# Second attention and expert product of an inducing-point mixture-of-experts kernel: fp32 weights in 32-row tiles in place of a split into two block-diagonal halves

## The chip, the cores and the metric

The kernel runs on one core of a Trainium2 chip, in one launch. The metric is the device time in microseconds (us), as the median of several runs. One execution was taken by the hardware profiler; its durations are the ones used here. Engines are named as the profile names them: PE (TensorE, matrix products), PEld (its weight loads), DVE (VectorE), ACT (ScalarE), POOL (GpSimd), SP (SyncE, which issues the loads and stores).

## The reference, cut to what matters

```python
B, N, m, C = (4, 11456, 32, 128)          # x: B x N x C, inducing: m x C
def mab(q, kv):
    s = scale * (q @ kv.transpose(0, 2, 1))
    s = s - s.max(-1, keepdims=True)
    a = np.exp(s)
    a /= a.sum(-1, keepdims=True) + 1e-09
    return a @ kv
h = mab(I, x)                             # first attention: 32 inducing points over all tokens
out = mab(x, h)                           # second attention: every token over the 32 rows of h
...
logits = out @ w_gate                     # E = 8 experts, D = 128, F = 1024
expert_idx = np.argmax(logits, axis=1)
gate_w = softmax(logits)[arange, expert_idx]
y = gate_w * (np.maximum(out @ w1[e], 0.0) @ w2[e])    # e = the token's expert
```

All tensors are fp32. The output has 45824 rows of 128. Where all tokens of a batch choose one expert and no hidden unit changes its sign over them, the expert is a fixed matrix: y = gate * (a @ L). The kernel computes in this form, proves both conditions on the chip, and has a general path behind them.

## The kernel before, in words

Each of the four batches is cut into G = 6 groups: five of 16 tiles (a tile is 128 tokens, one per partition) and a last one of 10 (8 and a tail of 2). `p1(i)` (from L389) does the first attention of group i, `chain(b)` (from L480) joins a batch's groups into h and prepares its expert, and `p2(i)` (from L603) does the second attention and the expert for group i.

`p1`: each x tile is transposed on PE (L400) and copied to `xT` (L403, through the helper at L313). Scores come from four fp32 products side by side, each into 32 of the 128 output partitions (L416), then the maximum (L423, L427, L430), the exponential (L434), a 32 x 32 block transpose on DVE (L438) and the sum over tokens, again four products side by side (L445).

`chain`: h is normalised and transposed to `hT` (L511 to L515), the expert is chosen, its weights are fetched by an indirect DMA (L531), and out of them comes L, the 32 x 128 matrix with y = gate * (a @ L). Nine router columns join it, so that one product gives 128 columns of y, 8 logits and the sum of the weights: `WY` = 137. L590 spreads L over the partitions with `selq` into two block-diagonal halves `[128, 2, 137]`, and L593 and L594 split that into `Lh` (fp32r, the rounded part) and `Ll` (the rest). In the last batch the nine router columns stand apart, in `rr` (L556), since gates are wanted there before the expert is known.

`p2`: scores (L612), a block transpose (L615), maximum (L617), difference (L619) and exponential (L623) leave the unnormalised weights `sd`: per partition 16 tokens by 32. These are split into `eh[..., 0]`, rounded to fp32r (the copy of L627), and `eh[..., 1]`, the rest (the subtraction of L629, POOL or DVE). A pair of tiles, rounded and rest, fills 128 columns, so a group has 8 transposes (L642), whose results go to SBUF as `eT` in two copies of 512 columns (L644). For each pair `my` (L652) runs two products of 274 columns, with `Lh` (L653) and with `Ll` (L654): the rounded and the rest are summed over the 128 rows, and the block diagonal keeps the two tiles of the pair apart. In the first three batches each pair goes to `ys` (L695), `gates` (from L720) makes 1 / (sum * sum of exponentials), and L708 or L706 scales four tiles at a time into `yo`, which SP stores (L716). In the last batch a product with `rr` (L648) gives logits first (`sp_`, then `st` by an addition, L665), the products of 256 columns leave PSUM scaled (L686, L688), or through `ya` and POOL (L677, L679) for the first `XQ[g]` quads, and stores go out per four tiles. In the last batch the products of the later quads wait for the gates (L673).

The order of work is not written out by hand. Every operation is recorded in a `Plan` (L137) with the engines that could run it, a rough cost on each, the tiles it reads and writes, and a key. `emit` (L166) takes the operation that can start first, adding a bias per kind of operation (`BIAS`, L59); within `WINDOW` ns the smaller key wins (L249). PSUM is 8 banks handed out as they come free (`pick`, L230); SBUF tiles have as many slots as `BUFS` (L60) says. The result is a fixed order of instructions on each engine.

Of the kernel before, what the change touches and what calls it, by code (L numbers as in the profile page):

```python
# [59 lines left out]
BUFS = {"w1e": 1, "w2e": 1, "x": 6, "xT": 7, "eT": 1, "eh": 3, "sd": 6, "a": 1, "aT": 1, "ys": 2, "yo": 2}  # L60
# [3 lines left out]
def inducing_moe_kernel(ctx: ExitStack, tc: tile.TileContext, x, inducing, w_gate, w1, w2, out):  # L64
    nc = tc.nc
# [17 lines left out]
    ident_r = consts.tile([128, 128], F32R, name="ident_r")  # L83
    dve.tensor_copy(ident_r, ident)
# [14 lines left out]
    # selq[:, q]: the columns of sel4 whose r has r % 2 == q  # L99
    selq = consts.tile([128, 2, 128], F32, name="selq")  # L100
    dve.memset(selq, 0.0)
    for r in range(4):
        dve.tensor_copy(selq[:, r % 2, 32 * r:32 * r + 32], sel4[:, 32 * r:32 * r + 32])
    # mq[:, q]: the rows whose block r has r % 2 == q
    mq = consts.tile([128, 2], F32, name="mq")
    dve.memset(mq, 0.0)
    for r in range(4):
        dve.memset(mq[32 * r:32 * r + 32, r % 2:r % 2 + 1], 1.0)
    # far: 0 where sel4 is 1, else far below everything
# [10 lines left out]
    # per batch state that outlives the pipeline  # L120
# [3 lines left out]
    far_ = consts.tile([128, B * G], F32, name="far_")     # the largest logit_j - logit_e of a group, per partition  # L124
# [12 lines left out]
class Plan:  # L137
    """Orders the recorded operations over the engines: a list schedule with rough costs.

    An operation is given with the engines that could run it and its cost in ns on each.  It waits  # L140
    for the earlier writers of what it reads and for the earlier readers of what it writes.  A tile
    is allocated by its first writer: the slot of its tag (SBUF) or the bank (PSUM) that has been free for longest.
    """

    @staticmethod
    def edge(a, b):
        """ns from the end of an operation on engine a to the start of one on b that waits for it"""
        if a == "sp" or b == "sp":
            return 1200
        return 197 if a == "pe" else 185 if b == "pe" else 142  # L150

    WINDOW = 20

    def __init__(self):
        self.ops, self.tiles, self.pull = [], {}, []
# [4 lines left out]
    def op(self, engs, fn, r=(), w=(), key=0.0, hold=(), pull=0.0):  # L160
# [3 lines left out]
        self.pull.append(pull)  # L164

    def emit(self, bufs, banks, run):  # L166
# [39 lines left out]
        def slots(i):  # L206
            """the last users of the slots that operation i opens; None if not yet known"""
            t = []
            for x in self.ops[i][3] + self.ops[i][5]:
# [3 lines left out]
                if tag == "bank":  # L213
                    k = pick()
                    if k is None:
                        return None
# [694 lines left out]
```

## Time and profile before

| what | value |
|---|---|
| median of 3 runs | 239.0 us |
| lowest and highest run | 238.43 and 242.09 us |
| span of the profiled execution, first to last instruction | 239.8 us |
| PE, DVE, ACT, POOL busy, of the span | 88%, 81%, 70%, 44% |
| granted TensorE clock, mean | 0.970 |
| moved by DMA | 51.62 MB, 215 GB/s on the mean |

No other time is given for the profiled execution, so its span stands for its own time; it lies 0.8 us above the median and between the lowest and the highest run. Busy times of PE include the modelled tail of each burst, so the step from one start to the next on the timeline says more of what PE can do. The granted clock is the mean of a stretch between its two levels, 1.2 and 2.4 GHz, as a share of the higher.

### The profile page before, as it was taken

To read this page: it belongs to the slowest core of one execution; us is meant where nothing else is said; L and a number is where in the kernel's file an instruction comes from. 1 tells how busy PE (TensorE), PEld (TensorE's weight loads), DVE (VectorE), ACT (ScalarE), POOL (GpSimd) and SP (SyncE) were. 2 spreads that over 40 slices of the span, in tenths; PEclk is the share of its full clock that TensorE was granted. 3 is DMA by queue.
4 is the path that set the end of the run, shared out by engine and by line. 5 is a ranking of instruction groups with operands and counts; after the bars stand their busy time and mean duration, and the time that the engine had idled before them with its cause. 6 is when DMAs were issued, how large, how long until landed. Compare 5 with 4: busy or idle time off the path is not lost.

```text
span 239.8 us, 6157 instructions
## 1 busy us (share of the span) xinstructions
PE 211.9 (88%) x2245; PEld 154.7 (65%) x2245; DVE 194.9 (81%) x608; ACT 168.9 (70%) x444; POOL 105.3 (44%) x115
## 2 busy tenths in 40 slices
PE   8599999989988999898998999999999988598460
PEld 5366765567946756666777656668676555598460
DVE  5124477998799799899897989999999999979950
ACT  3278754879946899798866897688986868577310
POOL 2000002242364446193582558295556868645400
PEclk9999999999999999999999999999999999889766
DMA  6995795941549574857569671425404724475872
GB/s 197 352 406 205 269 361 185 306 168 53 175 174 342 213 284 150 305 189 316 178 230 403 210 251 68 179 87 195 175 3 175 242 111 178 176 257 212 316 259 59
DMA packets 12310, 51.62 MB, mean 215 GB/s; under 512 B 1616, under 2 KB 2672, under 8 KB 7920
## 3 DMA queue, kind: packets, MB, share of 16 engines
q1 hardware_dynamic: 11120, 46.95, 53.1%
q0 software_dynamic: 1152, 4.19, 5.5%
q8 instruction: 20, 0.33, 0.6%
q14 instruction: 18, 0.15, 0.2%
HBM read 27.68 MB, written 23.46 MB: 213 GB/s over the span
## 4 chain that ended last, share of the span: by engine, by line
PE 43%; DVE 39%; ACT 6%; DMA 4%; issue 4%; SPq 1%; POOL 0%; ACTq 0%; DVEq 0%
PE b L400 8%; PE b L653 8%; PE b L654 6%; PE b L445 5%; DVE sd L619 4%; PE b L416 4%; DMA x<-in_x_dram 4%; DVE yo L708 4%; PE b L612 4%; DVE sd L615 3%; PE b L642 3%; DVE mx L423 3%; DVE mx L617 3%; DVE aT L438 2%; ACT xT L313 2%
## 5 line engine op out<-in xcount | busy, mean ns | idle before, releaser
L708 POOL TENSOR_TENSOR yo<-ys,gs 128x512 f32<-128x512 f32 (+1 forms) x48 | 53.4, 1131 | 17.7 <-DVE gs L739 7.6
L313 ACT COPY xT<-b 128x512 f32<-128x512 f32 (+1 forms) x92 | 48.4, 588 | 16.8 <-PE b L400 15.6
L400 PE MATMUL b<-ident,x 128*128 128x128 f32 x352 | 48.3, 281 | 2.9 <-DMA x<-in_x_dram 2.9
L400 PEld LDWEIGHTS b<-ident,x 128*128 128x128 f32 x352 | 40.2, 145 | 13.1 <-issue 5.4
L629 POOL TENSOR_TENSOR eh<-sd,eh 128x512 fp32r<-128x512 f32 (+1 forms) x24 | 30.1, 1257 | 33.6 <-ACT eh L313 15.7
L313 ACT COPY ys<-b 128x274 f32<-128x274 f32 x111 | 36.4, 403 | 8.1 <-PE b L654 6.3
L653 PE MATMUL b<-Lh,eT 128*128 128x274 f32 x135 | 39.9, 319 | 2.0 <-DVE eT L313 1.4
L654 PE MATMUL b<-Ll,eT 128*128 128x274 f32 x135 | 36.0, 291 | 0.0
L653 PEld LDWEIGHTS b<-Lh,eT 128*128 128x128 f32 x135 | 25.8, 191 | 12.8 <-issue 5.1
L654 PEld LDWEIGHTS b<-Ll,eT 128*128 128x128 f32 x135 | 25.7, 191 | 0.0
L416 PE MATMUL b<-xT,IT 128*32 128x512 f32 (+2 forms) x192 | 24.1, 571 | 0.7 <-ACT xT L313 0.6
L445 PE MATMUL b<-x,aT 128*32 128x128 f32 x704 | 24.1, 275 | 0.2 <-DVE nb L430 0.2
L612 PE MATMUL b<-xT,hT 128*32 128x512 f32 (+1 forms) x192 | 23.7, 576 | 0.0
L531 POOL DMA_INDIRECT w1e<-in_moe_w_dram,idx x4 | 4.3, 1075 | 42.1 <-DVE idx L525 40.4
L619 DVE CUSTOM_DVE_ANT_0 sd<-mx,sd 128x512 f32<-128x512 f32 (+1 forms) x24 | 21.9, 913 | 0.1
L445 PEld LDWEIGHTS b<-x,aT 128*32 128x32 f32 x704 | 18.2, 109 | 5.1 <-issue 2.9
L642 PE MATMUL b<-ident_r,eh 128*128 128x128 f32 x180 | 19.7, 250 | 1.1 <-POOL eh L629 0.7
L642 PEld LDWEIGHTS b<-ident_r,eh 128*128 128x128 f32 x180 | 17.2, 140 | 4.6 <-issue 1.8
L423 DVE TENSOR_REDUCE mx<-b 128x1 f32<-128x512 f32 (+1 forms) x24 | 15.3, 639 | 5.7 <-PE b L416 5.5
L438 DVE STREAM_TRANSPOSE aT<-a 128x512 f32<-128x512 f32 (+1 forms) x24 | 16.1, 669 | 4.1 <-ACT a L434 3.7
L434 ACT ACTIVATE a<-b,nb 128x512 f32<-128x512 f32 (+1 forms) x24 | 16.2, 674 | 3.1 <-DVE nb L430 3.0
L653 PE MATMUL b<-Lh,x 128*128 128x256 f32 x45 | 15.2, 356 | 2.0 <-ACT x L313 2.0
(208 smaller groups left out, 391.6 us busy)
## 6 DMA issues: line engine op xcount, KB each, us to landing
x<-in_x_dram SPq DMA_DIRECT2D x19, 1024.0 KB, 6.4
out_dram<-yo SPq DMA_DIRECT2D x15, 1024.0 KB, 4.3
out_dram<-ys SPq DMA_DIRECT2D x12, 256.0 KB, 2.8
out_dram<-yo SPq DMA_DIRECT2D x10, 256.0 KB, 2.2
x<-in_x_dram SPq DMA_DIRECT2D x4, 512.0 KB, 6.2
out_dram<-yo SPq DMA_DIRECT2D x3, 512.0 KB, 3.1
x<-in_x_dram SPq DMA_DIRECT2D x4, 256.0 KB, 3.2
xtail<-in_x_dram SPq DMA_DIRECT2D x4, 64.0 KB, 6.4
```

The lines of the kernel that those rows point to most:

```text
L313: (eng.copy if eng is nc.scalar else eng.tensor_copy)(out, in_)
L400: e.transpose(T[t][:, k, :], xtile(i, t0 + k), ident) for k in range(n)],
L416: e.matmul(T[t][32 * k:32 * k + 32, :ends[k]], IT, T[xT][:, k, :ends[k]], start=True, stop=True) for k in range(4)],
L423: e.tensor_reduce(T[mx], T[t][:, :nt], axis=AX.XY, op=OP.max)
L445: e.matmul(T[th][32 * k:32 * k + 32, :], T[aT][:n, q + k], xtile(i, q + k)[:n], start=q == 0, stop=q + k + 4 >= nt)
L612: e.matmul(T[tS][32 * k:32 * k + 32, :nt], hT, T[xT][:, k, :nt], start=True, stop=True) for k in range(4)],
L619: plan.op({"dve": vec(w) + 10}, lambda e: e.tensor_tensor_reduce(out=T[sd][:, :nt, :], in0=T[mx][:, :nt].unsqueeze(2).to_broadcast([128, n ...
L629: plan.op(Alt("lo" + late, pool=40 + 2.33 * w, dve=vec(w)), lambda e: e.tensor_sub(T[eh][:, :npair, 1], ev(), T[eh][:, :npair, 0].bitcast( ...
L642: e.transpose(T[t][:, a - a0, :], T[eh][:, a].rearrange("p x q m -> p (x q m)"), ident_r)
L653: e.matmul(t, T[eT][:, a, :], T[Lh], start=True, stop=False)
L654: e.matmul(t, T[eT][:, a, :], T[Ll], start=False, stop=True)
L708: e.tensor_mul(T[yo][:, t0:t0 + n], yv()[:, t0:t0 + n, :C], T[gs][:, t0:t0 + n].unsqueeze(2).to_broadcast([128, n, C]))
```

## The change

- `sd` is no longer split: `eh` with its copy and its subtraction goes. Four tiles of fp32 weights (4 x 32 = 128 columns) are transposed at once, so a group has 4 transposes in place of 8, into one PSUM bank, and one copy to `eT` in place of two (the group of 10 has 3 transposes and two smaller copies). These transposes take the key K2[2] that the split had, in place of K2[3]. `eT` has 6 slots of 4 x 128 in place of 1 of 8 x 128 beside the input's slots; `sd` has 4 in place of 6, `ys` 3 in place of 2.
- L is spread over four row blocks of 32 by one product with `sel4` and copied once, in fp32. `Lh`, `Ll`, `selq` and `ident_r` go.
- The last products are fp32, with 32 rows of `eT` as weights and 32 rows of L moving, one per tile: four side by side for a quad of tiles, each into a bank of its own. In the first three batches two quads are done at a time into four banks, and each bank (2 tiles, 4 apart) is copied to `ys` by itself; the last batch does all quads of a group into four banks.
- In the last batch `rr` becomes 128 x 4 x 9 fp32, the logits need no addition, products wait for the gates in the last group alone, and a scaled unit is every fourth tile, so each store of the group waits for all four units.
- The planner: `WINDOW` 20 becomes 100; a change of kind of product on PE (0 full, 1 four outputs side by side, 2 four row blocks) is booked at `SWITCH` = 95 ns; the last products may take banks 4 to 7 only, and while one of them is ready, everything else takes banks 0 to 3; some operations now hold a slot earlier (`hold`), and two score tiles at most are open (`sv`). A quad of the scaling on DVE is booked at 70 + 230 n in place of 70 + 1.05 x 128 n. `BIAS` is as it was.

```diff
+        def pick(x, taken=()):
+            allowed = range(4, banks) if x[0] == "y" else range(4) if any(self.mode[j] == 2 for j in ready) else range(banks)
+            free = [k for k in allowed if not bank_used[k] and k not in taken]
...
-        t7 = ps(("c7", b), [128, 2, LW])
-        on({"pe": 500}, lambda e: [e.matmul(T[t7][:, q], v["selq"][:, q, :], T[lq][:, :LW], start=True, stop=True)
-                                   for q in range(2)], [lq], [t7])
-        Lh, Ll = small("Lh", [128, 2, LW], F32R), small("Ll", [128, 2, LW], F32R)
-        on(Alt("gq", act=acc(2 * LW), dve=vec(2 * LW)), lambda e: copy(e, T[Lh], T[t7], nc), [t7], [Lh])
-        on({"dve": vec(2 * LW)}, lambda e: e.tensor_sub(T[Ll], T[t7], T[Lh].bitcast(F32)), [t7, Lh], [Ll])
+        t7, L = ps(("c7", b), [128, LW]), small("L", [128, LW])
+        on({"pe": 240}, lambda e: e.matmul(T[t7], sel4, T[lq][:, :LW], start=True, stop=True), [lq], [t7])
+        on(Alt("gq", act=acc(LW), dve=vec(LW)), lambda e: copy(e, T[L], T[t7], nc), [t7], [L])
...
-        plan.op(Alt("eh" + late, dve=vec(w, 0.53), act=acc(w) + 40), lambda e: copy(e, T[eh][:, :npair, 0], ev(), nc),
-                r=[sd], w=[eh], key=base + K2[2])
-        plan.op(Alt("lo" + late, pool=40 + 2.33 * w, dve=vec(w)), lambda e: e.tensor_sub(
-            T[eh][:, :npair, 1], ev(), T[eh][:, :npair, 0].bitcast(F32)), r=[sd, eh], w=[eh], key=base + K2[2])
...
+        nq = (nt + 3) // 4
+        eT = new(("eT", i), "eT", [128, 4, 128])
...
+        plan.op({"pe": 109 * nq}, lambda e, t=t: [
+            e.transpose(T[t][:rows(a), a, :], T[sd][:, 4 * a:min(4 * a + 4, nt)].rearrange("p t m -> p (t m)"), ident)
+            for a in range(nq)], r=[sd], w=[t], key=base + K2[2], hold=[eT])
...
+        def products(q0, q1, width):
...
+            for k in range(4):
+                own = [a for a in range(q0, q1) if 4 * a + k < nt]
+                if own:
+                    t.append(ps(("y", i, q0, k), [128, q1 - q0, width]))
...
+                for a in range(q0, q1):
+                    for k in range(min(4, nt - 4 * a)):
+                        e.matmul(T[t[k]][:, a - q0, :], T[eT][32 * k:32 * k + 32, a, :], T[L][32 * k:32 * k + 32, :width],
+                                 start=True, stop=True)
...
-            for a in range(npair):
-                t = ps(("y", i, a), [128, 2, WY])
-                plan.op({"pe": 235}, lambda e, t=t, a=a: my(e, T[t], a), r=[(eT, a // 4 * 4), Lh, Ll], w=[t],
-                        key=base + K2[4], hold=[eT])
-                plan.op(Alt("ys", act=acc(276), dve=vec(276)), lambda e, t=t, a=a: copy(e, T[ys][:, a], T[t], nc),
-                        r=[t], w=[ys, (ys, a)], key=base + K2[4])
+            for q0 in range(0, nq, 2):
+                q1 = min(q0 + 2, nq)
+                ts, ns, f = products(q0, q1, WY)
+                plan.op({"pe": 245 * (q1 - q0)}, f, r=[eT, L], w=ts, key=base + K2[4], mode=2, hold=[ys])
+                for k, (t, n) in enumerate(zip(ts, ns)):
+                    plan.op(Alt("ys", act=acc(WY * n), dve=vec(WY * n)), lambda e, t=t, n=n, t0=4 * q0 + k: copy(
+                        e, T[ys][:, t0:t0 + 4 * n - 3:4], T[t][:, :n], nc), r=[t], w=[ys, (ys, q0, k)], key=base + K2[4])
...
-                plan.op(Alt("yo", dve=vec(128 * n), pool=22 + 245 * n, act=293 * n), scale, r=Y + [gs, yo], w=[(yo, t0)],
+                plan.op(Alt("yo", dve=70 + 230 * n, pool=22 + 245 * n, act=293 * n), scale, r=Y + [gs, yo], w=[(yo, t0)],
```

## Rows read from the trace of the kernel before

**Rows 1.** The page, busy time of each engine over the span.
```profile
PE 211.9 (88%) x2245; PEld 154.7 (65%) x2245; DVE 194.9 (81%) x608; ACT 168.9 (70%) x444; POOL 105.3 (44%) x115
```

**Rows 2.** Windows by stage: length, busy us per engine, clock, DMA share, GB/s.
```profile
40.00:200.00 160.00, 152.11 (x1686) 107.54 (x1678) 148.22 (x450) 128.74 (x344) 87.08 (x88) 1.00 0.54 197
200.00:220.00 20.00, 15.87 (x127) 14.59 (x124) 18.18 (x53) 14.00 (x37) 13.44 (x14) 0.91 0.50 192
220.00:239.80 19.80, 8.66 (x52) 8.03 (x51) 10.69 (x37) 4.27 (x14) 3.15 (x3) 0.72 0.63 227
```

**Rows 3.** Timeline of PE, last products and the product that spreads L: start, us.
```profile
61.11 0.29 PE L653 MATMUL b<-Lh,eT 128*128 128x274 f32 x1
...
61.74 0.29 PE L654 MATMUL b<-Ll,eT 128*128 128x274 f32 x1
...
95.11 0.73 PE L590 MATMUL b<-lq,selq 128*128 128x137 f32 x4
95.60 0.38 PE L653 MATMUL b<-Lh,eT 128*128 128x274 f32 x1
```

**Rows 4.** Timeline of PE, four products side by side.
```profile
103.03 1.06 PE L445 MATMUL b<-x,aT 128*32 128x128 f32 x32
104.01 1.09 PE L400 MATMUL b<-ident,x 128*128 128x128 f32 x8
...
106.65 1.06 PE L612 MATMUL b<-xT,hT 128*32 128x512 f32 x8
107.54 1.04 PE L416 MATMUL b<-xT,IT 128*32 128x512 f32 x8
```

**Rows 5.** Timeline of PE, transposes and changes of kind.
```profile
84.73 0.88 PE L642 MATMUL b<-ident_r,eh 128*128 128x128 f32 x8
85.44 1.93 PE L400 MATMUL b<-ident,x 128*128 128x128 f32 x16
87.31 1.06 PE L612 MATMUL b<-xT,hT 128*32 128x512 f32 x8
88.30 0.62 PE L642 MATMUL b<-ident_r,eh 128*128 128x128 f32 x5
```

**Rows 6.** Windows of tile eh: PE, PEld, DVE, ACT, POOL, clock, DMA share, GB/s.
```profile
0.00:40.00 40.00, 0.00 (x0) 0.00 (x0) 0.00 (x0) 0.00 (x0) 0.00 (x0) 1.00 0.82 295
40.00:200.00 160.00, 16.63 (x151) 14.49 (x151) 2.17 (x5) 9.32 (x15) 24.96 (x20) 1.00 0.54 197
```

**Rows 7.** Windows of tile eT, then of Lh: PE, PEld, DVE, ACT, and so on.
```profile
40.00:200.00 160.00, 44.94 (x270) 36.66 (x270) 9.97 (x15) 11.01 (x21) 1.00 0.54 197
...
40.00:200.00 160.00, 39.93 (x135) 25.75 (x135) 2.19 (x5) 0.41 (x1) 1.00 0.54 197
```

**Rows 8.** Groups by line, shapes apart: the scaling into yo, the copies to ys.
```profile
L708 POOL TENSOR_TENSOR yo<-ys,gs 128x512 f32<-128x512 f32 x45 | 51.2, 1156 | 17.7 <-DVE gs L739 7.6 <-issue 7.1 <-POOL yo L708 1.2
...
L313 ACT COPY ys<-b 128x274 f32<-128x274 f32 x111 | 36.4, 403 | 8.1 <-PE b L654 6.3 <-PE b L416 0.8
...
L708 DVE TENSOR_TENSOR yo<-ys,gs 128x512 f32<-128x512 f32 x12 | 13.2, 1116 | 0.1
L706 ACT ACTIVATE yo<-ys,gs 128x128 f32<-128x128 f32 x36 | 11.5, 397 | 0.0
```

**Rows 9.** Timeline of all engines, the last batch: L, gates, last products, stores.
```profile
202.77 0.41 DVE L594 TENSOR_TENSOR Ll<-b,Lh 128x256 fp32r<-128x256 f32 x1
...
226.69 0.19 PE L770 MATMUL b<-cs,ones 128*1 128x1 f32 x2 [3.05 <-DVE gs+_4_3743 L737]
226.81 0.58 PE L653 MATMUL b<-Lh,x 128*128 128x256 f32 x1
...
231.46 0.41 PE L654 MATMUL b<-Ll,x 128*128 128x256 f32 x1
...
231.76 2.09 SPq L716 DMA_DIRECT2D out_dram<-yo  x4
231.91 0.62 ACT L686 ACTIVATE yo<-b,gs+_5_3757 128x128 f32<-128x128 f32 x2 [5.18 <-PE b L654]
```

More of the change, by code (lines that the diff above doesn't have):

```diff
@@ L98, in inducing_moe_kernel @@
         dve.tensor_add(sel4, sel4, s0)
-    selq = consts.tile([128, 2, 128], F32, name="selq")
-    dve.memset(selq, 0.0)
+    m4 = consts.tile([128, 4], F32, name="m4")
+    dve.memset(m4, 0.0)
     for r in range(4):
[L103 to L108, printed above, removed]
+        dve.memset(m4[32 * r:32 * r + 32, r:r + 1], 1.0)
     far = consts.tile([128, 128], F32, name="far")
@@ L203, in emit @@
         clock = {"pe": 1100.0, "dve": 5300.0, "act": 2000.0, "sp": 1800.0}
-        ready, cold, busy = {i for i in range(n) if not need[i]}, 0.0, []
+        ready, cold, busy, mode = {i for i in range(n) if not need[i]}, 0.0, [], 0
         def slots(i):
-            t = []
+            t, taken, more = [], [], []
             for x in self.ops[i][3] + self.ops[i][5]:
@@ L213, in slots, with slot @@
                 if tag == "bank":
-                    k = pick()
+                    k = pick(x, taken)
                     if k is None:
                         return None
+                    taken.append(k)
                     t += last[k]
                 else:
-                    k = slot(tag) if nxt[tag] == turn[x] else None
+                    k = slot(tag, [u for g, u in more if g == tag]) if nxt[tag] + sum(g == tag for g, _ in more) == turn[x] else None
                     if k is None:
                         return None
+                    more.append((tag, k))
                     t += users.get(holder[tag][k], ())
             return t
-        def slot(tag):
-            free = [(free_at[tag][k], k) for k, y in enumerate(holder[tag]) if y is None or not left[y]]
+        def slot(tag, taken=()):
+            free = [(free_at[tag][k], k) for k, y in enumerate(holder[tag]) if (y is None or not left[y]) and k not in taken]
             return min(free)[1] if free else None
-        def pick():
-            free = [k for k in range(banks) if not bank_used[k]]
+        def pick(x, taken=()):
+            allowed = range(4, banks) if x[0] == "y" else range(4) if any(self.mode[j] == 2 for j in ready) else range(banks)
+            free = [k for k in allowed if not bank_used[k] and k not in taken]
             return min(free, key=lambda k: bank_free[k]) if free else None
@@ L242, in emit @@
                         c *= 1.015
-                    st = max([clock.get(e, 0.0)] + [done[p] + self.edge(on[p], e) for p in s0]
+                    free = clock.get(e, 0.0) + (self.SWITCH if e == "pe" and self.mode[i] != mode else 0)
+                    st = max([free] + [done[p] + self.edge(on[p], e) for p in s0]
                              + [done[p] + self.edge(on[p], e) for p in preds[i]])
@@ L413, in p1 @@
         t = ps(("s", i), [128, 16, 32])
+        sv = ("sv", i)
+        bufs["sv"] = 2
+        plan.tile(sv, "sv", lambda k: None)
         ends = [nt] * 4 if g < G - 1 else [nt, nt, nt - 1, nt - 1]
@@ L446, in mh @@
                              start=q == 0, stop=q + k + 4 >= nt)
-        plan.op({"pe": 74 * nt}, mh, r=[aT] + xnames(i), w=[th], key=base + K1[3], pull=pull)
+        plan.op({"pe": 55 * nt + 40}, mh, r=[aT] + xnames(i), w=[th], key=base + K1[3], pull=pull, mode=1, hold=[hp])
         if g == G - 2:
@@ L632, in p2 @@
[L632 removed]
+        nq = (nt + 3) // 4
+        eT = new(("eT", i), "eT", [128, 4, 128])
         last = b == B - 1
         if last:
[L635 removed]
+            tr = ps(("tr", i), [128, 4, 36])
         else:
[L637 to L649 removed]
@@ new lines, in keep @@
+        def keep(e, t=t):
+            full = nt // 4
+            copy(e, T[eT][:, :full], T[t][:, :full], nc)
+            if nt % 4:
+                copy(e, T[eT][:rows(full), full], T[t][:rows(full), full], nc)
+        plan.op(Alt("eT" + late, act=acc(128 * nq), dve=vec(128 * nq)), keep, r=[t], w=[eT], key=base + K2[3])
+        if last:
+            plan.op({"pe": 220 * nq}, lambda e: [
+                e.matmul(T[tr][:, a, :9 * rows(a) // 32], T[eT][:rows(a), a, :],
+                         T["rr", b][:rows(a), :rows(a) // 32].rearrange("p r w -> p (r w)"), start=True, stop=True)
+                for a in range(nq)], r=[eT, ("rr", b)], w=[tr], key=base + K2[3])
@@ L668, in p2 @@
[L668 to L676 removed]
+            plan.op(Alt("gq", act=acc(9 * nt), dve=vec(9 * nt)), lambda e: copy(
+                e, T[st][:, :nt], T[tr].rearrange("p a (r w) -> p (a r) w", w=9)[:, :nt], nc),
+                    r=[tr], w=[st], key=base + K2[3])
@@ new lines, in p2 @@
+            gs = gates(i, nt, lambda: T[st], 0, [st], [], base + K2[3], "+")
+            ts, ns, f = products(0, nq, C)
+            yas = [new(("ya", i, k), "ya", [128, 4, C], n=3) for k in range(XQ[g])]
+            plan.op({"pe": 230 * nq}, f, r=[eT, L] + [gs] * (XQ[g] == 0), w=ts, key=base + K2[4], mode=2, hold=[yo] + yas)
+            for k, (t, n) in enumerate(zip(ts, ns)):
+                own = lambda tile, k=k, n=n: T[tile][:, k:4 * n - 3 + k:4]
+                gb = lambda k=k, n=n: T[gs][:, k:4 * n - 3 + k:4].unsqueeze(2).to_broadcast([128, n, C])
+                if k < XQ[g]:
+                    ya = yas[k]
@@ L716, in p2 @@
                 plan.op({"sp": 182.5 * (u1 - u0)}, lambda e, p0=p0, p1=p1, u0=u0, u1=u1, dr=dr[:, u0 - t0:u1 - t0]: e.dma_start(
-                    out=dr, in_=T[yo][p0:p1, u0:u1, :]), r=[(yo, k) for k in range(u0 // 4 * 4, u1, 4)], w=[("out", i, u0)],
+                    out=dr, in_=T[yo][p0:p1, u0:u1, :]), r=[(yo, k) for k in (range(min(4, nt)) if last else range(u0 // 4 * 4, u1, 4))], w=[("out", i, u0)],
                     key=key, hold=[yo])
```

106 lines of the change are left out of this document (41 added, 65 removed).

## The prediction

> **What bounds the kernel now.** I read the page first: PE is busy for 88% of the span, DVE for 81%, ACT for 70%, POOL for 44% [rows 1]. A share over the span hides the stages, so the windows come next. The stretch from 40 to 200 us holds the whole second attention of the first three batches beside first attention: PE is busy for 152.1 of 160 us (95%), DVE for 148.2 (93%), ACT for 128.7 (80%), POOL for 87.1 [rows 2]. Two engines are near full there, so a gain needs both to get lighter. Ahead of 40 us no instruction on `eh` runs [rows 6], so that stretch stays. Behind 200 us the last batch is left: DVE is busy for 18.2 of the first 20 us, and the rest thins out [rows 2]. Third, the timeline of PE gives steps from start to start; the duration of one record has the tail of its burst in it and would count the same time twice.
>
> **Prices on PE.** Between the first and the sixth record of a run of last products lie 0.63 us: 0.126 us a product of 274 columns [rows 3]. A quad of tiles takes two pairs with two products each: 0.50 us. After the change it takes four fp32 products of 137 columns, and such a product stands in this trace: L590 makes two, of 128 rows, in four records; from its start to the next product pass 0.49 us, 0.245 us each [rows 3]. If four of them with 32 rows each run truly side by side, a quad takes 0.245 us; if not at all, 0.98 us. The nearest rows are the products with four outputs side by side: L612 with 512 columns takes 0.89 us for all four, where four times 512/137 of 0.245 us would be 3.7; L445 makes 16 products of 128 columns in 0.98 us [rows 4]. So four at a time is real for tiles that split the outputs; no row here splits the rows of the array and keeps 128 outputs. I take 0.245 us, since the rows beside it show no loss, and keep 0.98 us as the other end.
>
> A page would put the price between: the Trainium skill ("TensorE: Matmul & The Clock Gate", Measured speedup vs the span model) measured 3.07 times, not 4, for four row tiles. By that a quad is 4 x 0.245 / 3.07 = 0.32 us, and the forecast below would be some 5 us higher; no run here shows it yet.
>
> **The stage from 40 to 200 us, on PE.** Last products: 270 records [rows 7] by 0.126 are 33.9 us. In their place stand 23 quads a batch (five groups of 4, one of 3), 69 in three, by 0.245: 16.9 us. That frees 17.0 us. Transposes: 151 records [rows 6] by 0.089 us (eight from 84.73 to 85.44 [rows 5]) are 13.4 us; after it the 69 quads, and 8 in place of the 16 that belong to the last batch, by 0.11 us (sixteen in 1.87 us less 0.10 for the change of kind [rows 5]) are 8.5 us: 4.9 us freed. What is added is changes of kind. L612 followed by a product of its own kind takes 0.89 us [rows 4], followed by a full one 0.99 [rows 5], so a change costs 0.10 us. Each group gets two bursts of row tiles, each with a change in and a change out: 18 groups x 2 x 2 x 0.10 = 7.2 us at most, less where a burst stands beside another, and nothing where one would have been paid anyway. I take 5. The net is 17.0 + 4.9 - 5 = 16.9 us, 11% of PE's 152.
>
> **The same stage on DVE, ACT and POOL.** The split goes whole: 2.2 us on DVE, 9.3 on ACT, 25.0 on POOL [rows 6]. The copies to `eT` halve: 10.0 + 11.0 us become about half [rows 7], 10.5 us freed. `Lh` and `Ll` cost 2.2 + 0.4 us for three batches [rows 7] and leave one copy each, about a third: 1.7 us. The copies to `ys` keep their columns, since eight copies of 274 a group remain. That is 2.2 + 9.3 + 10.5 + 1.7 = 23.7 of the 277 us of DVE and ACT, 9%. POOL has room for more: it loses 25 us, and a quad scaled there takes 1.16 us where DVE takes 1.12 and ACT four times 0.32 [rows 8]; 12 quads stood on DVE and 9 on ACT, 24.7 us. The planner's new cost for DVE (990 in place of 608 ns a quad) pushes them over. Half of it moving makes 12 us more, so DVE and ACT lose 13% together. Bounds: 9% with nothing moved, 17% with all.
>
> So PE gets 11% lighter and the other two 9 to 17%, in a stage where both fill over 90%. If it scaled with PE, 160 us would lose 17.8. I take 15, since the three chains of a batch (scores, hT, expert fetch, L) are latency and don't shrink; bounds 8 (if DVE sheds only its own part, 5% or so) and 24.
>
> What covers the edits put at nothing: the later place of the transposes (key K2[2]) is covered by `sd` with four slots and `eT` with six; a group's scores can run while an earlier group waits. Without that cover DVE's block transpose waits for a slot of `sd` and, behind it in DVE's fixed order, the maximum and the copies to `ys`, for which the four banks wait; one such wait is a transpose burst, a copy and two hand-overs, about 1.5 us. On the SP queue, loads and stores keep their size and number; only in the last batch do stores shift, below. POOL's queue, which also issues the expert's fetch, gets shorter. `WINDOW`, `sv` and the holds cost no instructions; by themselves they change only the order, between -2 and +4 us, taken as 0.
>
> **The last batch, 200 to 239.8 us.** L is there one step earlier: between L590 and the first use of `Ll` stands a copy and a subtraction on a crowded DVE, from 202.77 to 203.18, behind which PE waited [rows 9]: about 1 us. `st` no longer needs its additions, `rr` is made in fewer steps, POOL's split no longer runs beside DVE: with DVE busy for 18.2 of 20 us there, I take 2 us. At the end PE stood 3.05 us for the gates of the last groups, and then made 22 products in 4.65 us, 0.22 us each, at the lower clock, since the granted clock is 0.72 in this window [rows 2, 9]. After the change only the last group's three quads wait: 0.74 us at the full clock, 1.5 at the lower. But the group ahead of it then holds the four banks until its gates are there and its four units are scaled, and every store waits for all four units of its group, where the last stores now go out at 231.76 us while ACT still scales [rows 9]. I let the one pay for the other: 0, bounds -3 and +3. The tail: -3 us, bounds -8 and +3.
>
> **Sum.** 239.8 - 15 - 3 = 221.8 us by the profiled execution; the median of the runs shown lies 0.8 lower, so 221.0.
>
> **Rivals.** (1) *Weights are loaded one after another.* Each row tile is a product of its own with 128 columns of weights, loaded twice, as L590's four records for two products show. A quad has eight loads where four stood. What the trace shows of a load of 128 fp32 columns is that one and its transposing product take 0.11 us [rows 5] and a record of L590 0.122; if loads of different row blocks can't overlap, a quad takes at least 8 x 0.11 = 0.88 us. The stage then gains 69 x (0.50 - 0.88) = -26.2, + 4.9 - 5: PE gets 26 us more on an engine that is 95% full, and the last batch 23 x 0.38 = 9, of which some 4 show: 239 + 30 = 269 us. It decides from 0.50 us a quad on; at that price the gain of PE is nothing. For it: no row splits the rows of the array. Against it: the products with four outputs at once have loads too, and lose nothing; those are of 32 columns each, so the test is weak.
>
> A page speaks for this rival: by the Trainium skill ("TensorE: Matmul & The Clock Gate", LDWEIGHTS) a load's time goes with its columns, and one of 32 rows takes as long as one of 128. Another speaks against it ("TensorEngine Tiling (Array Packing)", Key Properties): different tiles load weights and multiply in parallel. I weigh them by the rows with four outputs, which fit the second.
>
> (2) *Banks take it back.* A half group's products need four free banks at once, and the rest has four while they are ready. A half group leaves by four copies of 0.40 us [rows 8] on two engines, 0.8 us, and two hand-overs. If PE stood 0.5 us at each of 36 half groups, 18 us would be gone: 239 us. For it: `Plan` had eight banks for all. Against it: PE has other work ready in nearly all of this stage.
>
> (3) *DVE stays the bound.* Most of what goes stood on ACT and POOL: DVE alone sheds 2.2 + 5 + 1.4 us, 6% of its 148. If the scaling stays where it is, the stage shrinks by 8 and the tail by 1: 230 us.
>
> **How the numbers follow.** The forecast has 0.66, rival 3 has 0.12, rival 2 0.11, rival 1 0.11. The forecast's own range is 208 to 230 us (its bounds of stage and tail, not all at one end). To leave no more than 2 in 10 out, the range reaches over rivals 3 and 2 partly: 206 to 239. Within 2% of before (234.2 to 243.8 us) is about what a measurement of this kernel can't tell from no change. Faster by more: 0.66 + 0.11 of rival 3 = 0.77; within 2%: 0.11 (rival 2 and the upper edge of 3, less its slower side); slower: rival 1 and a little of rival 2, 0.12.
>
> **What would show it.** Right: a quad's four products start within some 0.25 us of the next quad's; PE's busy time below 195 us and POOL's at or above 80, with DVE's quads of L708 fewer than 12; the stretch with second attention shorter by some 15 us at a granted clock of 1.00. If PE rests more, the clock may fall there too: in the last window it stands at 0.72 and a product takes 0.22 us in place of 0.126 [rows 2, 3, 9]; that would take part of the gain. Wrong: steps near 0.9 us a quad (rival 1); PE idle ahead of the last products with copies to `ys` as releaser (rival 2); DVE above 95% with PE below 85% (rival 3).

## The result and the profile after

The changed kernel takes 232.64 us (median of four runs, 231.54 to 234.33) where the kernel before takes 240.55 beside it: a ratio of 0.9705, with a 95% interval of 0.9625 to 0.9786. The forecast was 221.0. The direction was right, and less than half of the gain came. Ratios go by undisturbed runs alone, medians by all runs.

The page of the kernel after, its busy times and its clock by slices, stands against [rows 1]:

```profile
PE 203.3 (87%) x2510; PEld 135.4 (58%) x2510; DVE 175.0 (75%) x583; ACT 156.9 (67%) x429; POOL 75.8 (33%) x92
...
PEclk9979998599999999999999999999997998556655
```

PE lost 8.6 us of busy time, DVE 19.9, ACT 12.0, POOL 29.5. The clock row shows what no share shows: TensorE was slowed near the start (slices of 5.8 us), for a moment near 176 us, and from about 195 us on.

To place the gain I cut each span where the last L is spread over the partitions (the product of L590 before, L597 after) and where the last gates end (L739, L757). First the kernel before, then after, then the changed kernel once more (the control, below); columns as in [rows 2].

```profile
53.90:200.10 146.20, 139.22 (x1515) 99.90 (x1515) 134.44 (x412) 117.98 (x321) 81.23 (x83) 1.00 0.53 196
200.10:227.50 27.40, 20.05 (x158) 18.54 (x155) 25.35 (x82) 17.55 (x49) 15.86 (x17) 0.90 0.61 230
227.50:239.80 12.30, 4.37 (x21) 4.08 (x20) 3.46 (x5) 0.62 (x2) 0.62 (x1) 0.64 0.48 164
```
```profile
58.40:190.20 131.80, 123.20 (x1675) 77.19 (x1673) 116.60 (x385) 103.75 (x296) 56.71 (x63) 0.99 0.59 214
190.20:220.10 29.90, 26.51 (x269) 22.26 (x269) 27.09 (x93) 19.82 (x60) 15.37 (x17) 0.66 0.56 212
220.10:232.50 12.40, 0.87 (x15) 0.57 (x11) 1.22 (x3) 0.88 (x3) 0.00 (x0) 0.50 0.55 194
```
```profile
54.20:185.30 131.10, 121.53 (x1675) 77.00 (x1673) 116.18 (x385) 103.77 (x296) 56.65 (x63) 1.00 0.59 215
185.30:214.70 29.40, 26.18 (x270) 22.14 (x270) 26.98 (x93) 19.82 (x60) 15.87 (x17) 0.70 0.58 220
214.70:227.00 12.30, 0.95 (x15) 0.65 (x13) 1.24 (x4) 0.89 (x3) 0.00 (x0) 0.50 0.53 185
```

Read down the second column. From the first L to the last, 146.2 us became 131.8 and 131.1: the gain is here, and whole. From the last L to the last gates, 27.4 became 29.9 and 29.4: a loss, with DVE busy for 91 to 93% of it in all three, and TensorE's clock at 0.66 and 0.70 where it was 0.90 before. Behind the gates the length stayed but not the content: PE's 4.4 us and DVE's 3.5 became 0.9 and 1.2, and what fills the time now is the stores, for which the DMA engines were full (share 1.02) while the last of that work ended, kernel after:

```profile
220.00:222.00 2.00, 0.97 (x16) 0.67 (x15) 0.99 (x4) 0.88 (x3) 0.00 (x0) 0.50 1.02 374
222.00:224.00 2.00, 0.00 (x0) 0.00 (x0) 0.28 (x1) 0.00 (x0) 0.00 (x0) 0.50 1.02 375
```

Ahead of the first L (53.9 us before) one run of the changed kernel lost 4.5 us and the other 0.3, though the instructions are the same: that goes with the clock, which stood at 0.91 up to there in the one and at 1.00 in the other.

Last products on the timeline of PE, kernel after (start, duration), for [rows 3] and [rows 4]:

```profile
63.97 0.28 PE L435 MATMUL b<-ident,mx 128*128 128x128 f32 x1
64.37 0.75 PE L671 MATMUL b<-L,eT 32*128 32x137 f32 x16
65.05 1.60 PE L616 MATMUL b<-xT,hT 128*32 128x512 f32 x16
66.59 0.75 PE L671 MATMUL b<-L,eT 32*128 32x137 f32 x16
67.27 1.09 PE L404 MATMUL b<-ident,x 128*128 128x128 f32 x8
```

A product of fp32 shows as two records, so sixteen records are two quads of four; from start to next start pass 0.68 us with the changes of kind in it. What PE waited for longest at the last products stands among its waits (total, times, longest):

```profile
PE b L519 <- DVE sw L516: 3.2, 3, 1.2
PE b L654 <- ACT eT L317: 2.9, 3, 1.6
PE b L404 <- DMA x<-in_x_dram: 2.5, 1, 2.5
...
PE b L671 <- DVE ys L317: 0.6, 1, 0.6
...
PE b L671 <- ACT ys L317: 0.2, 1, 0.2
```

For copies to `ys`, which free the banks of the last products, PE stood 0.8 us in all. The groups that scale `yo` answer to [rows 8]:

```profile
L726 POOL TENSOR_TENSOR yo<-ys,gs 128x512 f32<-128x512 f32 x47 | 51.5, 1115 | 31.4 <-issue 14.2 <-DVE gs L757 6.3 <-DVE ab L602 3.4
...
L724 ACT ACTIVATE yo<-ys,gs 128x128 f32<-128x128 f32 x56 | 17.8, 399 | 0.9 <-ACT ys L317 0.8 <-DVE gs L755 0.2
...
L726 DVE TENSOR_TENSOR yo<-ys,gs 128x512 f32<-128x512 f32 x5 | 5.0, 998 | 0.0
```

DVE gave away 7 of its 12 quads, but ACT took 5 of them (9 to 14) and POOL 2 (45 to 47).

### The profile page after: what moved, and what is told of

Same layout as the page of the kernel before. It is cut to its first block, busy times and chain, and to the rows that moved or that the text cites. A ratio compares the mean times of both kernels' runs of the same rounds, so it can differ in the third digit from the quotient of the medians.

```text
span 232.5 us, 6577 instructions
## 1 busy us (share of the span) xinstructions
PE 203.3 (87%) x2510; PEld 135.4 (58%) x2510; DVE 175.0 (75%) x583; ACT 156.9 (67%) x429; POOL 75.8 (33%) x92
## 4 chain that ended last, share of the span: by engine, by line
PE 45%; DVE 36%; ACT 4%; issue 4%; DMA 3%; POOL 2%; SPq 1%; DVEq 0%; POOLq 0%; ACTq 0%
PE b L404 13%; PE b L453 7%; PE b L424 6%; PE b L671 6%; PE b L616 5%; DVE ys L317 4%; DMA x<-in_x_dram 3%; DVE sd L618 3%; DVE mx L620 3%; DVE sd L622 3%; DVE ld L749 2%; PE b L643 2%; DVE aT L446 2%; DVE mx L431 2%; PE b L435 1%
## 5 line engine op out<-in xcount | busy, mean ns | idle before, releaser
L726 POOL TENSOR_TENSOR yo<-ys,gs 128x512 f32<-128x512 f32 (+1 forms) x50 | 54.1, 1102 | 31.4 <-issue 14.2
L404 PE MATMUL b<-ident,x 128*128 128x128 f32 x352 | 50.2, 289 | 3.8 <-DMA x<-in_x_dram 2.5
L404 PEld LDWEIGHTS b<-ident,x 128*128 128x128 f32 x352 | 41.4, 148 | 17.1 <-issue 7.5
L671 PE MATMUL b<-L,eT 32*128 32x137 f32 (+1 forms) x720 | 40.6, 325 | 1.1 <-DVE ys L317 0.6
L671 PEld LDWEIGHTS b<-L,eT 32*128 32x128 f32 x720 | 31.1, 206 | 17.7 <-issue 6.5
L317 ACT COPY ys<-b 128x274 f32<-128x274 f32 (+1 forms) x97 | 31.3, 388 | 9.0 <-PE b L671 7.4
L616 PE MATMUL b<-xT,hT 128*32 128x512 f32 (+1 forms) x192 | 26.6, 650 | 0.8 <-DVE sd L618 0.8
L424 PE MATMUL b<-xT,IT 128*32 128x512 f32 (+2 forms) x192 | 24.1, 573 | 0.5 <-ACT xT L317 0.5
L746 POOL TENSOR_SCALAR s<-ys 128x16 f32<-128x16 f32 (+1 forms) x16 | 5.4, 340 | 57.2 <-DVE hp L484 24.1
L618 DVE STREAM_TRANSPOSE sd<-b 128x512 f32<-128x512 f32 (+1 forms) x24 | 16.0, 668 | 4.9 <-PE b L616 4.9
L622 DVE CUSTOM_DVE_ANT_0 sd<-mx,sd 128x512 f32<-128x512 f32 (+1 forms) x24 | 19.0, 792 | 0.1
L724 ACT ACTIVATE yo<-ys,gs 128x128 f32<-128x128 f32 x56 | 17.8, 399 | 0.9 <-ACT ys L317 0.8
L539 POOL DMA_INDIRECT w1e<-in_moe_w_dram,idx x4 | 4.4, 1101 | 41.1 <-DVE ei L535 39.7
L317 DVE COPY ys<-b 128x274 f32<-128x274 f32 x41 | 16.7, 427 | 0.8 <-PE b L671 0.7
L626 ACT ACTIVATE sd<-sd 128x512 f32<-128x512 f32 (+1 forms) x24 | 14.5, 615 | 3.1 <-DVE dst L622 3.0
L643 PE MATMUL b<-ident,sd 128*128 128x128 f32 (+1 forms) x92 | 15.3, 303 | 0.2 <-ACT sd L626 0.2
```

The costliest lines, as they stand in the source:

```text
L317: (eng.copy if eng is nc.scalar else eng.tensor_copy)(out, in_)
L404: e.transpose(T[t][:, k, :], xtile(i, t0 + k), ident) for k in range(n)],
L424: e.matmul(T[t][32 * k:32 * k + 32, :ends[k]], IT, T[xT][:, k, :ends[k]], start=True, stop=True) for k in range(4)],
L616: e.matmul(T[tS][32 * k:32 * k + 32, :nt], hT, T[xT][:, k, :nt], start=True, stop=True) for k in range(4)],
L618: plan.op({"dve": vec(w)}, lambda e: e.transpose(T[s2][:, :nt], T[tS][:, :nt]), r=[tS], w=[s2], key=base + K2[0])
L622: plan.op({"dve": vec(w) + 10}, lambda e: e.tensor_tensor_reduce(out=T[sd][:, :nt, :], in0=T[mx][:, :nt].unsqueeze(2).to_broadcast([128, n ...
```

## The experiments

My theory after the result: the stage gained what was forecast; the rest went to a slow clock at the start in some runs, and to DVE work that now lies behind the last L. Rivals: the slow clock at the end costs it; the stores do; a quad is dearer than it looks.

Ratios are to the kernel before, run beside each of four groups: e1, e2, e3, e4; c0, e5, e6, e7; b1, e8, e9, e10; e11, e12, e13. A ratio compares best within its group. Edits are to the changed kernel where nothing else is said.

**The start kept busy (e1), the end (e2), both (e3), the kernel before (b1).** Products of a matrix of ones, overwritten at once by the real ones, stand ahead of the places where PE rests early, the second group's transposes and the product that makes h transposed in batches 0, 1 and 3 (e1), and ahead of the logits in the last batch (e2).

```diff
 # e1: transposes of L404; product of L519
+ [e.matmul(T[t][:, :2], ones, ones.unsqueeze(1).to_broadcast([128, 2, 128]), start=True, stop=True)
+  for _ in range(4 if i == 1 and t0 == 0 else 0)] +
+ [e.matmul(T[t2b][:, :128], ones, ones, start=True, stop=True) for _ in range(4 if b in (0, 1, 3) else 0)] +
 # e2: logits of L654
+ [e.matmul(T[tr][:, :, :32], ones, ones.rearrange("p (a c) -> p a c", a=4), start=True, stop=True)
+  for _ in range(8 if g == 1 else 4)] +
```

> The changed kernel with the same order of work and idle TensorE time filled at two places ahead of the last batch: four fp32 products of 256 columns ahead of the first transposes of the second group (PE stood 2.5 us for the input there and ran at 1.2 GHz from 12 to 15.3 us), and four of 128 columns ahead of the product that makes h^T in batches 0, 1 and 3 (PE stood some 1 us there and ran at 1.2 GHz from 39.3 to 46.2 and from 175.9 to 178.9 us). Theory clock: the missing gain is PE time at the lower level; the head gets 1.6 + 3.4 + 1.5 us back at most, so 227 to 230 us in place of 232.6, and the granted clock of 0 to 190 us is near 1.00. Theory DVE: the chain and DVE hold the pace, PE at half speed was slack: 232 to 234 us at a higher clock.

> The changed kernel with the same order and four fp32 products of 128 columns (eight for the second group) ahead of each logit product of the last batch, where PE stood 0.7 to 1.6 us for the copy of eT. Theory clock: PE stays at 2.4 GHz from 196 to 213 us, its products there take half, and the tail gets 5 to 8 us shorter: 225 to 228 us. Theory DVE: the tail is paced by DVE, the gates and the stores: 232 to 235 us, the fill being paid for nothing.

> Both fills together. Theory clock: about 221 us, what was forecast, with a mean granted clock above 0.97. Theory DVE: 232 to 236 us.

> The kernel before with the start fill alone (four fp32 products of 256 columns ahead of the second group's first transposes, where PE stood 2.2 us for the input). Theory: its clock stays at 2.4 GHz ahead of 200 us anyway in its profile, so the median gains at most what single runs lose by a dip: ratio 0.99 to 1.00. If the kernel before loses to the clock as the changed one does, ratio 0.98 or less, and part of the gain of the head fill has nothing to do with the change.

e1 took 228.55 us, 0.9443 [0.9392, 0.9495]; e2 231.26, 0.9528 [0.9453, 0.9603]; e3 229.34, 0.9494 [0.9428, 0.9559]. The kernel before with the first of e1's two edits (b1) took 242.02, 0.9981 [0.994, 1.0023]: no difference. The windows from 9 to 20 and from 40 to 47 us, after, then the control, then e1:

```profile
9.00:20.00 11.00, 8.76 (x86) 7.23 (x90) 2.48 (x7) 5.67 (x12) 0.00 (x0) 0.84 0.86 336
...
40.00:47.00 7.00, 7.00 (x39) 4.00 (x36) 5.09 (x19) 1.43 (x4) 2.11 (x2) 0.56 0.88 301
```
```profile
9.00:20.00 11.00, 8.48 (x92) 5.87 (x93) 2.74 (x8) 6.55 (x14) 0.00 (x0) 1.00 0.96 372
...
40.00:47.00 7.00, 7.00 (x65) 4.11 (x61) 6.89 (x20) 4.68 (x10) 2.12 (x2) 1.00 0.78 293
```
```profile
9.00:20.00 11.00, 11.00 (x112) 8.29 (x109) 3.57 (x9) 7.24 (x16) 0.00 (x0) 1.00 0.98 387
```

Between 40 and 47 us PE is full in the first two rows, but at a clock of 0.56 it got 39 records done where the same kernel at 1.00 did 65. PE had stood 2.52 us for an input and 1.23 us for DVE ahead of the two falls (the longest waits on L404 and L519 above). But the control stood nearly as long at the same places, 2.25 and 1.23 us, and kept its clock, so the wait alone doesn't bring the fall. What the start costs is the clock and not the order of work.

The end is another matter. From last L to last gates the clock was 0.97 in e2 and 0.93 in e3, 0.66 in the kernel after, and the stretch took 29.2, 30.3 and 29.9 us:

```profile
188.00:217.20 29.20, 25.72 (x327) 22.63 (x326) 24.74 (x91) 19.49 (x59) 12.95 (x15) 0.97 0.59 224
```
```profile
185.70:216.00 30.30, 26.67 (x325) 23.08 (x325) 26.69 (x93) 19.73 (x60) 15.41 (x17) 0.93 0.57 219
```

Holding the clock up in this way gains nothing. It doesn't show that a slow TensorE is free there: the added products alone keep PE busy for 7.7 us of the stretch in e2 and 8.0 in e3, so PE is busy as long as without them (25.7 and 26.7 us for 26.5).

Runs of one order of work at two clocks tell more. e7 is e5 (both below) with the busy start, e13 is e4 with it, and b1 is the kernel before with a part of it; behind the last L each pair has the same instructions in the same order. The same stretch in e5, then e7, then b1, whose partner is the kernel before above:

```profile
188.60:216.40 27.80, 23.32 (x270) 19.58 (x270) 25.82 (x91) 19.24 (x59) 13.26 (x15) 0.80 0.63 241
```
```profile
187.20:217.80 30.60, 25.88 (x270) 21.98 (x270) 25.82 (x92) 19.62 (x59) 13.42 (x15) 0.66 0.61 233
```
```profile
198.55:228.46 29.91, 22.54 (x158) 21.01 (x155) 26.16 (x82) 17.85 (x49) 15.94 (x17) 0.79 0.56 211
```

With the same 25.82 us of DVE work, e7 takes 2.8 us longer than e5 at a clock lower by 0.14. b1 takes 2.5 us longer than the kernel before (0.79 for 0.90), and e13 1.6 longer than e4 (31.0 us at 0.66, 29.4 at 0.77). These are single executions, but all three point one way: a slow clock in this stretch costs time, and the first rival stands.

**The changed kernel again (c0), and e1 again (e12).**

> The changed kernel again, beside the runs below, to read them against on one chip and to see how its granted clock moves from run to run. Ratio to the kernel before 0.96 to 0.98; where PE drops to 1.2 GHz may differ from the first profile, and a run in which it stays up ahead of 50 us should spread the first L (products with sel4) at 53 to 54 us in place of 58.

> The kernel whose start is kept busy, a second time. If the start's products keep the clock up by more than chance, the ratio to before is again 0.940 to 0.950 (about 228.5 us); if the first run of it was a lucky one, it lies at the changed kernel's 0.963 to 0.970 (232 us).

The control took 231.54 us, from 228.78 to 233.47: 0.9626 [0.9527, 0.9726]. Its profiled execution was the fastest of them, had no fall of the clock ahead of the last L, and its span (227.0) is that of e1 (226.9). e12 took 230.24, 0.9475 [0.9388, 0.9562]. The busy start stands at 0.944 and 0.948, the plain changed kernel at 0.971 and 0.963: 3.7 to 6.3 us. The intervals of e12 and the control overlap, so the size is rough. The profiles bear the cause out: ahead of the first L the clock is at 1.00 in all seven with the busy start (e1, e3, e7, e10 to e13), and at 0.91 to 0.97 in six of the eight without it.

**The last products twice (e4), and twice on e1 (e13); a second maximum on DVE in the same batches (e11, on e1).**

```diff
 # e4, e13
-                    for k in range(min(4, nt - 4 * a)):
+                    for k in [k for _ in range(2 if b < B - 1 else 1) for k in range(min(4, nt - 4 * a))]:
 # e11: maximum of L620
-  e.tensor_reduce(T[mx][:, :nt], T[s2][:, :nt], axis=AX.X, op=OP.max)
+  [e.tensor_reduce(T[mx][:, :nt], T[s2][:, :nt], axis=AX.X, op=OP.max) for _ in range(2 if b < B - 1 else 1)]
```

> The changed kernel, same order, with the last products of the first three batches issued twice over the same result (69 quads by 0.245 us, 17 us more on PE); nothing else is changed. Theory PE (PE is still the bound between 40 and 190 us): 245 to 250 us. Theory DVE (PE has slack there since the change): below 238 us. A quad that costs more than 0.5 us would show as over 265.

> The first 18 groups' maximum of the second attention made twice on DVE, some 0.65 us each: 11.7 us more of DVE work, nothing on PE. If PE alone sets the length of this stretch, DVE has slack and the time rises by at most 3 us over the unchanged kernel beside it. If DVE binds as PE does, it rises by 6 to 8 us; if DVE alone binds (rival 3 of the forecast), by 10 to 12 us.

> The last products of the first three batches issued twice: 69 quads by 0.245 us, 16.9 us more on PE alone. If PE alone binds, the time rises by 15 to 17 us over the unchanged kernel beside it; if PE and DVE share the bound, by 10 to 12 us as in the same edit on the changed kernel; if DVE alone binds, by at most 4 us.

e4 took 242.35 us, 0.994 [0.9878, 1.0003]; e13 240.31, 0.9866 [0.9769, 0.9964]; e11 238.07, 0.9772 [0.9662, 0.9883]. First L to last, e12, e11, e13:

```profile
54.00:185.30 131.30, 124.56 (x1690) 80.06 (x1688) 116.76 (x385) 104.09 (x296) 56.60 (x63) 1.00 0.59 214
```
```profile
56.30:194.60 138.30, 126.42 (x1691) 80.74 (x1689) 125.01 (x399) 104.56 (x296) 57.09 (x63) 1.00 0.55 202
```
```profile
54.30:197.60 143.30, 138.71 (x2215) 95.35 (x2213) 117.42 (x387) 103.93 (x296) 56.55 (x64) 1.00 0.54 197
```

PE got 14.2 us more in e13 and the stage grew by 12.0; DVE got 8.3 more in e11 and the stage grew by 7.0. Over e12 beside them, e13 is slower by 0.039 and e11 by 0.030 of the kernel before, 9.5 and 7.2 us. Each engine's extra work shows nearly whole, while the other has idle time, which fits a fixed order that hands the work back and forth: neither has slack to give. So both limits are at work, as the forecast took them, and rival 3 (DVE alone) falls. In e13 a burst of four quads is followed after 1.15 us where two take 0.68 (65.05 less 64.37 above): 0.235 us a quad, and 0.21 for the changes of kind around a burst.

```profile
60.20 1.22 PE L671 MATMUL b<-L,eT 32*128 32x137 f32 x32
61.35 1.60 PE L616 MATMUL b<-xT,hT 128*32 128x512 f32 x16
```

**More DVE work in the last batch alone (e9).**

```diff
-  e.tensor_reduce(T[mx][:, :nt], T[s2][:, :nt], axis=AX.X, op=OP.max)
+  [e.tensor_reduce(T[mx][:, :nt], T[s2][:, :nt], axis=AX.X, op=OP.max) for _ in range(2 if b == B - 1 else 1)]
```

> The changed kernel, same order, with the maximum over the 32 weights computed twice in the last batch (six reductions on DVE, 5 x 0.67 + 0.48 = 3.8 us). Theory DVE sets the tail: 3 to 4 us slower than the control, L of the last batch (product with sel4) at the same time, the way from there to the last gates some 33 us in place of 29.4. Theory clock or stores set the tail: below 1.5 us slower.

235.76 us, 0.9752 [0.9696, 0.9808]; by ratios 0.0126 or 3.0 us over the control, with an interval that overlaps it. In the profiles, with the same late first L (58.0 and 58.4 us), 3.8 us of added work put the last L 1.8 us later than in the kernel after (192.0 for 190.2), the last gates 3.4 (223.5 for 220.1) and the end 2.5 (235.0 for 232.5). The expectation had L at its old time and the whole delay behind it. About half of the added maxima ran ahead of the last L, in a stage whose clock was 0.97 in place of 0.99. So DVE work of the last batch counts; that DVE alone paces the end isn't shown. The groups of DVE between last L and last gates say what stands there. Kernel after, then before:

```profile
L622 DVE CUSTOM_DVE_ANT_0 sd<-mx,sd 128x512 f32<-128x512 f32 (+1 forms) x4 | 3.2, 795 | 0.0
L620 DVE TENSOR_REDUCE mx<-sd 128x16 f32<-128x512 f32 (+1 forms) x4 | 2.5, 624 | 0.0
L618 DVE STREAM_TRANSPOSE sd<-b 128x512 f32<-128x512 f32 (+1 forms) x3 | 1.9, 621 | 0.0
...
L704 DVE TENSOR_TENSOR ys<-b,gs+_4_3465 128x512 f32<-128x512 f32 x2 | 1.3, 681 | 0.0
L317 DVE COPY ys<-b 128x274 f32<-128x274 f32 x3 | 1.2, 435 | 0.0
```
```profile
L619 DVE CUSTOM_DVE_ANT_0 sd<-mx,sd 128x512 f32<-128x512 f32 (+1 forms) x3 | 2.7, 895 | 0.0
L617 DVE TENSOR_REDUCE mx<-sd 128x16 f32<-128x512 f32 (+1 forms) x3 | 1.7, 560 | 0.0
L665 DVE TENSOR_TENSOR st<-sp 128x144 f32<-128x144 f32 (+1 forms) x4 | 1.7, 418 | 0.0
...
L313 DVE CAST x<-b 128x512 fp32r<-128x512 f32 x2 | 1.3, 660 | 0.3 <-PE b L642 0.3
```

What was to go has gone: the additions into `st` (1.7 us), the casts into fp32r (1.3). But one group more of the last batch (L618 to L622: 0.7 + 0.8 + 0.5 us over before), three copies to `ys` (1.2) and more of the third batch's gates now lie behind the last L; and the scaling of the fifth group (1.3), which stood behind the last gates before, now stands ahead of them. In sum DVE has 27.09 us there in place of 25.35, and behind the gates 1.22 in place of 3.46: from the last L to the end 28.3 us where it had 28.8.

**Stores and units (e5, e7, e10).** In e5 a scaled unit of the last batch is four neighbouring tiles again, so a store waits for one unit and not four; e7 adds e1's edits to it. e10 is e1 with two quads a group through `ya` and POOL.

```diff
 # e5, e7: scores of the last batch read the tiles in the other order
+  T[xT][:, k].rearrange("c (r a) p -> c a r p", a=4) if con else T[xT][:, k, :nt]
...
-  r=[(yo, k) for k in (range(min(4, nt)) if last else range(u0 // 4 * 4, u1, 4))]
+  r=[(yo, k) for k in ([u0 // 4] if con else range(min(4, nt)) if last else range(u0 // 4 * 4, u1, 4))]
 # e10, on e1
-XQ = (1, 1, 1, 2, 1, 0)
+XQ = (2, 2, 2, 2, 2, 0)
```

> The changed kernel with the tiles of a quad in the last batch's first five groups taken four apart (scores written in that order), so that each scaled unit is four neighbouring tiles and each store waits for its own unit alone. Theory drain: the stores of the last groups pile up because each waits for four units; 3.6 us of the tail (11.5 us from the last product to the end, 7.9 before) come back in part: 2 to 3 us faster than the control, the way from last product to end 8.5 to 10 us. Theory bandwidth: the last 5.9 MB leave at what the DMA engines give, order is nothing: within 1 us of the control.

> Contiguous units and the fill at the head together. If both theories hold they add: the fill 3 to 4 us, the stores 2 to 3: 225 to 227 us, ratio to the kernel before 0.930 to 0.94. If the stores are a matter of bandwidth: as the head fill alone, ratio 0.944.

> The fill at the head, and in the last batch two of four units per group go through ACT and POOL in place of one (XQ = 2, 2, 2, 2, 2, 0): four units of 0.65 us less on DVE. Theory DVE sets the tail: 2 to 3 us faster than the head fill alone (ratio to the kernel before 0.944), ratio 0.932 to 0.937. Theory stores set the tail: as the head fill, 0.944, or slower, since a unit by ACT and POOL takes 0.6 + 1.05 us.

e5 took 230.53 us, 0.9595 [0.9483, 0.9707], beside the control's 0.9626: the same. e7 230.43, 0.9526 [0.943, 0.9622], no better than e1. e10 231.51, 0.9599 [0.9551, 0.9647], worse than e1. From last gates to the end e5 takes 11.2 us in place of 12.3; e11 and e13, whose stores wait for four units as ever, take 11.3 and 11.7. So the wait for four units is worth a microsecond at most; what the stores themselves take wasn't varied. e10 has 24.1 us of DVE work between last L and last gates where e12 has 27.1, yet the stretch is only 0.5 us shorter (28.8 for 29.3), and 14.5 follow to the end in place of 12.4: its expectation failed, which speaks against DVE alone.

**ACT loaded (e6) and the banks set free (e8).**

```diff
 # e6: behind the exponential of L626
+  e.copy(T[sd][:, :nt], T[sd][:, :nt])
 # e8
-  allowed = range(4, banks) if x[0] == "y" else range(4) if any(self.mode[j] == 2 for j in ready) else range(banks)
+  allowed = range(4, banks) if x[0] == "y" else range(banks)
```

> The changed kernel, same order, with the copy of the split put back on ACT (after the exponential a copy of the weights onto themselves, 24 of some 0.6 us, 14 us on ACT and in the chain to the transposes). Theory PE (PE is the bound for two thirds of the stage): ACT has slack, 1 to 3 us slower than the control. Theory shared bound (all three engines share the stage): 6 us or more slower.

> The changed kernel with the limit on the other products lifted: while last products are ready, everything else may take any of the eight banks again (the last products keep to banks 4 to 7); the planner makes a new order. Theory clock and tail (what was seen so far): banks cost nothing, within 2% of the control, 228 to 235 us. Rival banks: PE stood for banks, 5 us or more faster than the control.

e6 took 234.17 us, 0.9737 [0.9611, 0.9862], 2.7 us over the control by ratios, less than the two are uncertain: 11 us more on ACT (168.1 in place of 156.9) cost little, so ACT alone isn't the limit. e8 took 252.38, 1.0466 [1.0405, 1.0528], slower than the kernel before. Its timeline of PE at the end:

```profile
224.19 2.48 PE L671 MATMUL b<-L,eT 32*128 32x128 f32 x32
226.93 3.12 PE L671 MATMUL b<-L,eT 32*128 32x128 f32 x32 [0.27 <-ACT ya L317]
230.32 3.11 PE L671 MATMUL b<-L,eT 32*128 32x128 f32 x32 [0.28 <-ACT ya L317]
```

With no banks kept for them, all but one group of the last batch's products start when everything else is done, at 224.19 us (last L: 194.8), and run one group at a time to 239.24 at a clock of 0.50. So one line of the planner, with the order that comes of it, is worth 20 us; the forecast priced it only with "the order".

## Why the prediction was right or wrong

By the profiled execution the forecast was 239.8 - 15 - 3 = 221.8 us; it measured 232.5, 10.7 more. Start: +4.5 for 0. Stage, from the first L to the last: -14.4 for -15. From the last L on: +2.6 for -3 (39.7 us became 42.3). That is 4.5 + 0.6 + 5.6 = 10.7. Against the control (227.0) the start is off by 0.3 only, and the tail, 41.7 us, still by 5.0.

**Right: the price of a quad.** Forecast 0.245 us, measured 0.235; rival 1 falls. The figure from the Trainium skill ("TensorE: Matmul & The Clock Gate", Measured speedup vs the span model), 3.07 times for four row tiles of 512 columns, would make it 0.32, an estimate: this trace, with 137 columns, shows the full four times. The other page of the Trainium skill weighed there ("TensorEngine Tiling (Array Packing)", Key Properties), by which tiles load and multiply in parallel, agrees with the trace.

**Right: the stage.** 15 forecast, 14.4 and 15.1 measured, at the clock of 1.00 that was asked for (0.99 and 1.00). It doesn't always keep that clock: in e5, where it fell to 0.95, the stage took 136.0 us. PE lost 11.5% of its busy time between first and last L (139.2 to 123.2 us) where 11% was forecast. DVE and ACT together lost 12.7% there (252.4 to 220.4 us) where 13% was forecast. The way there was not as told: the quads of `yo` were to go to POOL, whose busy time was to stay at or above 80; it is 75.8, since ACT took most of them. "PE's busy time below 195" also failed: 203.3, of which the control shows 6 to be the clock (197.0). Rival 2's mechanism is absent as it stood: 0.8 us of waiting for `ys`.

**Wrong: "The tail: -3 us".** The step counted 1 us for an earlier L and 2 for the DVE work that goes, and put no price on TensorE's clock there. Both halves failed. From the last L to the end DVE had 0.5 us less work and not 2, since other work of the last two batches took the place of what went. That a stage which ends 14 us sooner pushed it there was read from the groups of instructions; no run tried it by itself. And the clock from last L to last gates fell from 0.90 to 0.66 (0.70 in the control), with PE busy for 26.5 us there in place of 20.1. The pairs of one order above lose 1.6 to 2.8 us to a fall of 0.11 to 0.14; at their rate a fall of 0.20 to 0.24 costs some 3 to 5 us (an estimate from the pairs). The forecast named a falling clock as a danger, with PE resting more, but gave it no price here.

How the 5.6 us divide between order and clock stays open, since no run held the clock up there without adding PE work. The +2.6 itself rests on one execution of the kernel before: in b1 the same order takes 42.2 us from the last L to the end, as much as the kernel after (42.3). So the change may have cost the tail nothing, but it didn't win the 3 us either. The 0 for waiting products against stores came out in its sum (12.4 us for 12.3).

**Wrong: "Ahead of 40 us no instruction on `eh` runs, so that stretch stays".** The instructions stay, the clock doesn't. At the start, too, the forecast gave the clock no price. It cost 4.5 us in the profiled execution, and the busy start wins back 3.7 to 6.3 by the ratios of e1 and e12. Why the kernel before escapes is open: its clock is at 1.00 in this stretch of the profiled run, its runs granted 0.94 to 0.97 on the whole, and products that fill its start change nothing (b1).

**Wrong, small: the offset.** In every run whose span and device time both stand, the device time is 1.7 to 2.1 us above the span, 1.8 in most. So the execution profiled before, with a span of 239.8, was one of some 241.6 us: not 0.8 above the median of 239.0 but 2.6. A device time forecast from it would be 223.6 and not 221.0.

Of the versions tried, e1 is the fastest (0.9443 [0.9392, 0.9495] and again 0.9475), faster than both kernels; e3 (0.9494) and e7 (0.9526) can't be told from it.

## What to carry to other kernels

When a change shortens a stage that hides the next one's work, list what the hidden work was and see what no longer fits: counting removed instructions alone, the forecast took 2 us off DVE's work in the tail where 0.5 went. Read the granted clock by slices in several runs before a stretch is called unchanged, and give its fall a price wherever PE will rest more. Added products that hold the clock up don't show what the clock costs where they stand in the way of other work; two runs of one order at different clocks do. Where PE waits early a few idle products are worth trying: here they win more than the whole forecast of the tail. Where an operation wants four banks at once, the rule that keeps them free is part of its price.

## What was not expected of the hardware

Four fp32 products of 32 rows and 137 columns run side by side at 0.235 us for all four, though each has its own load of weights. The clock can fall to its lower level at 12 us and again at 39 us of one run and stay at 2.4 GHz there in another of the same program; runs of this kernel differ by 5.5 us (228.78 at a mean of 0.934, 234.33 at 0.900). In the last batch the same instructions in the same order took 27.8 us at 0.80 and 30.6 at 0.66. And a busy PE didn't bring it back at once: from 40 to 47 us PE rested in no part of the window, and the mean was 0.56.
